# Seven products for eight in the out step of the last 1024 tokens, with a new order for the late third

## The chip, the cores and the metric

The kernel runs on one core of one Trainium2 chip. The metric is the device time of one execution in microseconds. Five engines run their own instruction streams side by side: TensorE (PE in the profile), VectorE (DVE), ScalarE (ACT), GpSimd (POOL) and SyncE (SP, which here only issues DMAs). They wait for one another through semaphores.

## The reference

An attention layer with a forgetting gate feeds a bilinear feed-forward layer. Batch 8, 8 heads, 576 positions, head dimension 64; 4608 tokens of 512 features, 1536 hidden units.

```python
scores = scale * np.matmul(q, k.transpose(0, 1, 3, 2))
cum = np.cumsum(np.log(np.clip(f, 0.0001, 1.0)), axis=-1)
scores = np.where(causal, -1e9, scores + cum[..., :, None] - cum[..., None, :])
attn = softmax(scores)                      # max taken off, summed, + 1e-9
x = np.matmul(attn, v)                      # -> (4608, 512), heads side by side
out = ((x @ w_a) * (x @ w_b)) @ w_out       # (512, 1536), (512, 1536), (1536, 512)
```

Inputs and output are float32; the kernel multiplies in float16 and sums in float32.

## The kernel before, in words

**Attention** goes batch by batch, two heads (a pair) at a time, 32 pairs t = 0 to 31. For a pair TensorE makes the scores into PSUM (tile `sc`), VectorE adds the decay and takes the row's extreme in one instruction (line 673, reading `sc` from PSUM and the tile `spread` from SBUF, writing `S`), ScalarE takes the exponential (700 to 704, tiles `PA` and `PB`), VectorE the reciprocal (712, 714), GpSimd multiplies by it in place (725, float16 in SBUF, the "norms"). SyncE transposes `PA` and `PB` by DMA into `PTA` and `PTB` (739), TensorE multiplies with v (768, 783, `pvx`), and VectorE or ScalarE casts the result into the tiles `xT`, which hold x transposed.

**The feed-forward layer** follows on tokens that are ready. The *in step* of a chunk (`ffn`) makes for each block of 128 hidden units `psa` and `psb` (x with w_a and w_b), ScalarE casts `psa` to `a`, VectorE multiplies (line 1072) to the float16 hidden tile `ht`. The *out step* (`out_step`, `ff_out`) multiplies 128 tokens' hidden tiles with w_out: 12 blocks of hidden units, each as two halves of 64 output rows side by side (line 74, `mm_halves`), 512 columns, into the PSUM tile `pso`. A copy to `osb` and a DMA to the output follow. The last 128 tokens go in three pieces of 256, 128 and 128 columns (`psz`).

**The last 1024 tokens** have another in step already, `winograd()`. Taking two halves of 512 tokens and two halves of the 512 features, x with w_a and w_b forms a two by two block product, done per block of hidden units in seven products of four matmuls of 512 columns (`product`, tiles `wg`, `wb`) for eight. It needs sums of the weights (`sub_w`, line 1218, 12 VectorE instructions on 128x1024 float16) and of x (`add_x`, line 1224, 8 of them on 128x512 float16), copies of partial products to SBUF (`snap`, lines 288 and 292, tiles `wu`, `wv`) and combinations (`combine`, line 1273): c11, c12, h2 and half of the c22 on VectorE, each with one input from PSUM; h1 and the other half of the c22 on GpSimd, both inputs from SBUF. h1 and h2 are the hidden tiles of the two halves of tokens (`hy`, `ht` and `hx`).

**Order.** Nothing is scheduled at run time. Each piece of work is an `Op`; the string `ORDER` lists all of them in the sequence in which they are recorded, which is each engine's instruction order; `CHOICE` names the engine where two could do an operation; `SLOTS` says which buffer of each ring a tile takes. An engine works strictly in its order and stops at an instruction whose inputs or buffer are not ready.

Of the kernel before, what the change touches and what calls it, by code (L numbers as in the profile page):

```python
# [9 lines left out]
FP32 = mybir.dt.float32  # L10
# [15 lines left out]
def kernel(  # L26
# [78 lines left out]
    def paddings():  # L105
# [37 lines left out]
        0110101010101001010101010101010010011010100101001000100010011011010011010100110101001101010101011010110  # L143
        ;a16:012012012012012012012012012012012102102120120120120102102102021021012012012102102102102102;bc:0120
        120120120120120120120120;ff:012301230132000312301201313123131023120221010121332030123012301230123012301
        3021320210123103103023103120321023102310230231032123123120323102103102132012301020201230213201320312031
        0321032102312312031203120123102310231021031231230132132132020310310320120312023102130213210320312031213
        0131030310132102013013012301303210310210310321320320132031023012301231203012301213021031212302301320123
        01320123103210321302130210321013201320;ht:0123456789abcd0123456789abcd0123456789ab01cd2345678a019b23cd4
        568017a29bd345c0168279a34bd015c2;n16:011010010110001010010101010101;n32:0120102102102102010202121220120  # L150
        110102121101202201201202102;nv:01010101;osb:010101010100101010101010101110101010;qd:0101010101010101010
        10101;sc:0101010101010101010101011010010101100010101011001001010110101010101101010101010101010010101110
        1100101010110010101110101010101010100101010101;st:01234510324510324510324510324510
# [41 lines left out]
    def packets(n, size):  # L195
        return n * PKT[size] / 16
# [1077 lines left out]

    PLAIN = range(0, 12, 2)

    def winograd():
# [24 lines left out]
        muls = [[], []]  # L1302
        hu = {}
        first = None
        for fb in range(12):
# [59 lines left out]
    for n in cuts:  # L1365
# [85 lines left out]
        1507-1509 1421 1450 1451 1414 1532 1436 1429 2100 1489 1490 1385 2102 1487 1371 1372 2104 1581 1452  # L1451
# [11 lines left out]
        2161 2159 2143 1691 1692 2211 1587 2162-2164 2166 2165 1649 2167 1543 2209 1530 1693 1602 1550 1594  # L1463
# [3 lines left out]
        1703 2216 2210 2213 2194 1651 1658 2197 2214 2198-2200 2212 1657 1660-1662 1701 1702 1704-1706 2202  # L1467
# [5 lines left out]
        2322 2307-2309 2326 2324 2310 2335 2351 2312 2338 2325 2328 2327 2329 2311 2313 2314 2317 2330 2341  # L1473
        2336 2332 2331 2334 2337 2318 2339 2340 2342 2344 2345 2316 2354 2315 2319 2333 2352 2353 2366 2346
        2355 2356 2369 2343 2357 2358 2348 2349 2347 2350 2372 2373 2360 2359 2367 2368 2363 2382 2361 2370
        2375 2371 2364 2362 2365 2397 2374 2376-2378 2398 2379 2381 2399 2383-2385 2400 2403 2401 2402 2388
        2386 2387 2201 2405 2404 2410 2413 2390 2389 2394 2406 2407 2391 2392 2380 2414 2411 2409 2395 2393
        2408 2415 2416 2418-2420 2417 2421 2423-2426 2422 2396 2428 2427 2412 2429 2430 2433 2434 2431 2432
        2435 2438 2436 2437 2439-2446 2448-2450 2453 2451 2454 2447 2452 2455-2462
# [3 lines left out]
        PPPPPPDDDAPPPPPPPPPAADAAAAADADDAAAAADADDADADDAADDDAADAADDDADADDAAAADADDAADAAADADDAAAAAAADDDAAAAAADAAADA  # L1483
        AAAADADAAAAAADADDAAAAAAADDDAAAAAADAAAAAAADADAAADAAAAAAADADAAAAAAAAA
# [46 lines left out]
```

## Time and profile before

| | |
|---|---|
| median of 3 runs | 397.29 us (396.17 to 397.76) |
| the profiled execution | 395.96 us, span of its instructions 393.9 us |
| granted TensorE clock | 1.00 |
| busy, TensorE / VectorE / ScalarE / GpSimd | 382.3 / 319.2 / 296.5 / 280.4 us |
| first block product of the last 1024 tokens (`wg`) | starts at 332.90 us |
| last matmul | ends near 391 us |

A row of the timeline is: start, duration (of a merged run of like instructions), engine, line, operation, output tile <- input tiles, shape, count, and in brackets the idle time before it and what ended that. A row of a group has the busy time, the mean of one instruction in ns, and the idle time before the group. A row of a table by stretches of time has its limits, its length, and for each engine the busy time with the number of instructions, then the granted clock, the DMA engines' share and GB/s. In the chain of waits, a row is the start, the time on the chain, engine, tile, line and count.

### The profile page before, as it was taken

What the parts mean: (1) busy time and instruction counts of PE and PEld (TensorE: products, weight loads), DVE (VectorE), ACT (ScalarE), POOL (GpSimd) and SP (SyncE); (2) the same over time, 40 slices, a digit from 0 to 9 for tenths busy, and PEclk for the clock granted to TensorE, in tenths of its full rate; (3) what the DMA queues carried; (4) which work ended last, traced back from release to release, by engine and by line L of the source; (5) the groups of instructions that cost most, each with busy time, mean ns of one, the idle gap of its engine ahead of it and who ended that gap; (6) DMA issues with size and microseconds to landing.
All of it is one profiled execution on the core that took longest, in us unless ns stands there. A gap on an engine that the chain in (4) does not pass through costs nothing.

```text
span 393.9 us, 14686 instructions
## 1 busy us (share of the span) xinstructions
PE 382.3 (97%) x5720; PEld 251.3 (64%) x5720; DVE 319.2 (81%) x1015; ACT 296.5 (75%) x817; POOL 280.4 (71%) x482
## 2 busy tenths in 40 slices
PE   7899999999999999999999999999999989999997
PEld 3557977969766665655555665555655677666665
DVE  7888898998997779788887798758998898989700
ACT  4998999999888878778988588789898662455221
POOL 8699677778877689884897779678976980357600
PEclk9999999999999999999999999999999999999999
DMA  7999999999999999999999999999999895100022
GB/s 125 265 188 173 153 147 232 231 289 284 188 233 245 219 285 211 263 236 266 256 229 264 256 227 213 260 270 229 207 203 223 185 139 137 55 1 2 2 108 107
DMA packets 147365, 76.87 MB, mean 195 GB/s; under 512 B 124384, under 2 KB 128352, under 8 KB 147296
## 3 DMA queue, kind: packets, MB, share of 16 engines
q1 hardware_dynamic: 132856, 68.72, 77.2%
q0 software_dynamic: 14256, 7.08, 14.6%
q8 instruction: 44, 0.72, 0.7%
q14 instruction: 25, 0.20, 0.2%
q10 hardware_dynamic: 184, 0.14, 0.1%
HBM read 52.05 MB, written 9.58 MB: 156 GB/s over the span
## 4 chain that ended last, share of the span: by engine, by line
PE 79%; DMA 7%; POOL 4%; DVE 4%; ACT 3%; issue 2%; DVEq 0%; ACTq 0%; POOLq 0%
PE pso L74 20%; PE psa L74 16%; PE psb L74 15%; PE wg L74 5%; PE wb L74 4%; PE sc L550 3%; PE pvx L768 3%; DMA PTB<-PB 2%; PE psT L358 2%; DMA wout<-in_moe_w_out_dram 2%; POOL PA L725 2%; PE sc L538 2%; ACT PA L704 2%; PE wake L74 2%; DVE S L673 2%
## 5 line engine op out<-in xcount | busy, mean ns | idle before, releaser
L673 DVE CUSTOM_DVE_ANT_0 S<-sc,spread 64x576 f32<-64x576 f32 (+4 forms) x232 | 125.4, 561 | 14.2 <-ACT PA L704 4.8
L725 POOL TENSOR_SCALAR PA<-PA,st 128x256 f16<-128x256 f16 (+2 forms) x180 | 85.6, 487 | 10.5 <-DVE st L714 7.5
L74 PE MATMUL psa<-xT,wa 128*64 128x512 f16 (+2 forms) x864 | 88.9, 333 | 1.7 <-DVE ht L1072 1.7
L74 PE MATMUL psb<-xT,wb 128*64 128x512 f16 (+2 forms) x864 | 88.7, 332 | 0.4 <-DVE ht L1072 0.2
L704 ACT ACTIVATE PA<-S,st 128x256 f16<-128x256 f32 (+2 forms) x168 | 84.1, 503 | 6.2 <-DVE st L673 5.7
L74 PE MATMUL pso<-wout,ht 128*64 128x512 f16 x696 | 85.5, 380 | 0.3 <-DMA wout<-in_moe_w_out_dram 0.3
L725 POOL TENSOR_SCALAR PB<-PB,st 128x512 f16<-128x512 f16 (+1 forms) x90 | 64.0, 719 | 23.4 <-DVE st L714 8.7
L74 PEld LDWEIGHTS <-wa 128*64 128x64 f16 x960 | 55.4, 110 | 26.3 <-issue 4.2
L74 PEld LDWEIGHTS <-wb 128*64 128x64 f16 x960 | 56.5, 110 | 24.3 <-issue 1.7
L288 ACT CAST a<-psa 128x512 f16<-128x512 f32 (+1 forms) x90 | 49.4, 551 | 18.1 <-PE psa L74 14.9
L1072 DVE TENSOR_TENSOR ht<-psb,a 128x512 f16<-128x512 f32 (+1 forms) x90 | 57.6, 649 | 6.2 <-PE psb L74 4.1
L74 PEld LDWEIGHTS <-ht 128*64 128x64 f16 x696 | 38.8, 110 | 27.9 <-issue 2.6
L704 ACT ACTIVATE PB<-S,st 128x512 f16<-128x512 f32 x56 | 40.2, 720 | 3.4 <-DVE st L673 2.9
L704 ACT ACTIVATION_READ_ACCUMULATOR PA<-S,st 128x1 f32 x168 | 31.9, 190 | 0.0
L700 ACT ACTIVATE PB<-S,st 128x576 f16<-128x576 f32 x28 | 21.7, 776 | 9.2 <-DMA PTB<-PB 3.6
L630 POOL TENSOR_SCALAR_AFFINE_SELECT spread<-spread 128x768 f32<-128x768 f32 x24 | 20.9, 871 | 10.7 <-DMA spread<-cum_d 10.3
L288 ACT COPY osb<-pso 128x512 f32<-128x512 f32 x28 | 16.3, 583 | 15.4 <-PE pso L74 15.4
L768 PEld LDWEIGHTS <-nv 128*64 128x64 f16 x640 | 22.0, 110 | 6.7 <-DMA PTA<-PA 2.1
L1273 POOL TENSOR_TENSOR hy<-wu 128x512 f16<-128x512 f32 x9 | 11.4, 1278 | 20.3 <-DVE wu L1273 20.3
L673 DVE CUSTOM_DVE_ANT_1 S<-sc,spread 128x256 f32<-128x256 f32 x48 | 19.7, 420 | 6.5 <-PE sc L538 1.9
L714 DVE RECIPROCAL st<-st 128x2 f32<-128x2 f32 x128 | 18.2, 156 | 7.4 <-ACT PA L704 3.8
L673 DVE DVE_READ_ACCUMULATOR2_ANT st<- 128x1 f32 (+1 forms) x280 | 22.9, 82 | 0.0
(136 smaller groups left out, 674.6 us busy)
## 6 DMA issues: line engine op xcount, KB each, us to landing
spread<-cum_d SPq DMA_DIRECT2D x24, 576.0 KB, 6.4
out_dram<-osb SPq DMA_DIRECT2D x35, 256.0 KB, 3.4
q<-in_q_dram SPq DMA_DIRECT2D x14, 576.0 KB, 5.3
k<-in_k_dram SPq DMA_DIRECT2D x14, 576.0 KB, 5.1
v<-in_v_dram SPq DMA_DIRECT2D x24, 256.0 KB, 6.0
wout<-in_moe_w_out_dram POOLq DMA_DIRECT2D x3, 512.0 KB, 8.0
nv<-in_v_dram POOLq DMA_DIRECT2D x8, 128.0 KB, 5.9
wa<-in_moe_w_a_dram POOLq DMA_DIRECT2D x2, 512.0 KB, 7.6
```

Source lines behind the costliest of these rows:

```text
L74: nc.tensor.matmul(out=out[r], lhsT=lhsT[:, r], rhs=rhs, **kw)
L288: nc.scalar.copy(out=out_, in_=in_)
L550: nc.tensor.matmul(out=dst, lhsT=lhsT, rhs=rhs, start=start, stop=stop, skip_group_check=True)
L630: nc.gpsimd.affine_select(out=c[:, :, 0:SM].rearrange("p h (j k) -> p h j k", k=128), in_=c[:, :, SM:2 * SM].rearrange("p h (j k) -> p h j ...
L673: nc.vector.tensor_tensor_reduce(out=o, in0=x, in1=y, scale=-1.0, scalar=3e38, op0=ADD, op1=MIN, accum_out=m)
L700: nc.scalar.activation(out=p_blocks(t, 4), in_=T[("s" if direct else "z", t, 4)], func=EXP, bias=st[:, 8:9], scale=sign, accum_out=st[:, 1 ...
L704: nc.scalar.activation(out=p_blocks(t, i)[:, :, h, :], in_=(T[("s", t, i)][:, h, :] if direct else T[("z", t, i)][:, h * n:h * n + n]).rea ...
L714: nc.vector.reciprocal(out=st[:, 20 + 2 * i:22 + 2 * i], in_=st[:, 10 + 2 * i:12 + 2 * i])
L725: VEC[e].tensor_scalar(out=p, in0=p, scalar1=st[:, c:c + 1], scalar2=1.0, op0=MUL, op1=MUL)
L768: nc.tensor.matmul(out=o[HP[h], 128 * i:128 * i + 128], lhsT=vt[:, j, pr + NP * h, :], rhs=pt[:, base_blk[i] + 2 * block_at(t, i, j) + h, ...
L1072: nc.vector.tensor_tensor(out=ht[:, 0:n_], in0=T.pop(("psb", t0, fbs))[:, 0:n_], in1=T.pop(("a16", t0, fbs))[:, 0:n_], op=MUL)
L1273: VEC[e].tensor_tensor(out=out_, in0=x, in1=y, op=op)
```

## The change

Three things are changed; `winograd()` and the loop over batches stay.

1. The out step of the last 1024 tokens becomes a two by two block product too: two halves of 512 tokens with two halves of the 512 output columns, over even and odd blocks of hidden units. For each of four blocks of 128 tokens (p, standing for a block in each half) there are seven products of 6 x 2 matmuls of 256 columns (`out_product`, Ops `vm1` to `vm7`). The weight differences (`sub_out`, tile `tw`: four of them in two pieces, 128x768 float16) and the sums of hidden tiles (`add_h`, Ops `sh0` to `sh3`: 24 on 128x512 float16, kept in the buffers of `spread` and, for `sh2`, in place) are VectorE's. Partial products are copied to SBUF (`o_snap`, tile `ou`), joined (`o_join`, 12 on 128x256 float32, one input from PSUM), copied (`o_copy`) and stored by rows of 512 columns; the very last block's lower row is stored in two pieces.
2. `out_step` is no longer called for these tokens, and the three-piece end (`last_out`) is gone with it.
3. `ORDER`, `CHOICE` and `SLOTS` are new from the softmax of pair 26 on. In `CHOICE`, three casts of `pvx` and two copies of `pso` go from VectorE to ScalarE, one copy of `kT` the other way, and in the last stage seven copies of partial products from VectorE to ScalarE.

```diff
+    def sub_out(e, k, j):
+        fs = slice(3 * j, 3 * j + 3)
...
+        t = [T[("tw", m)][:, fs, :] if ("tw", m) in T else None for m in range(4)]
+        x, y = ((w_out(0, fs, 1), w_out(0, fs, 0)), (w_out(1, fs, 1), t[0]),
+                (w_out(1, fs, 1), w_out(0, fs, 1)), (w_out(1, fs, 0), t[1]))[k]
+        VEC[e].tensor_tensor(out=t[k], in0=x, in1=y, op=SUB)
...
+    def add_h(e, k, f):
+        h = lambda i, j: T[("ht", TW[i], 2 * f + j)]
+        x, y = ((h, (1, 0)), (h_sum, (0, f)), (h, (0, 0)), (h, (0, 1)))[k], ((h, (1, 1)), (h, (0, 0)), (h, (1, 0)), (h_sum, (1, f)))[k]
+        x, y = x[0](*x[1]), y[0](*y[1])
+        VEC[e].tensor_tensor(out=h_sum(k, f), in0=x, in1=y, op=SUB if k else ADD)
+
+    def out_product(m, p):
...
+        for f in range(6):
+            x = {1: lambda: T[("ht", TW[0], 2 * f)], 2: lambda: T[("ht", TW[0], 2 * f + 1)], 3: lambda: h_sum(3, f),
+                 4: lambda: T[("ht", TW[1], 2 * f + 1)], 5: lambda: h_sum(0, f), 6: lambda: h_sum(1, f),
+                 7: lambda: h_sum(2, f)}[m]()[:, c]
...
+            mm_halves(o, x, w, start=(f == 0 and m in (1, 2, 5)), stop=(f == 5), skip_group_check=True)
...
+            m1 = mm(1, [])
+            s1 = cp(1)
+            m2 = mm(2, [])
+            j11 = join(11, [m2, s1])
+            m5 = mm(5, [])
+            s5 = cp(5)
+            m6 = mm(6, [s1])
+            s6 = cp(6)
+            m3 = mm(3, [s5])
+            j12 = join(12, [m3, s6, j11])
...
+            au.append(store(0, 0, 512, [j11, j12]))
+            m7 = mm(7, [s6])
+            j22 = join(22, [m7, s5])
...
+            m4 = mm(4, [j22])
...
-                muls[half].append((h, hu[key]))
-        for tb in range(8):
-            out_step(TW[0], tb, muls[tb // 4], 0.04 * TW[0])
+                hids[(half, fb)] = (h, hu[key])
+        out_products(hids)
```

VectorE's instructions in the last stage, before. L1273 are the combinations, L292 copies of partial products, L1218 the last weight difference of the in step.

```order
L1273 TENSOR_TENSOR hx<-wg,wv 128x512
L1218 TENSOR_TENSOR wb_77<-wb_77 128x2x512
L292 COPY wv<-wb 128x512
L1273 TENSOR_TENSOR wu<-wb,wu 128x512 x3
L1273 TENSOR_TENSOR wv<-wv,wg 128x512
L1273 TENSOR_TENSOR hx<-wg,wv 128x512 x2
L1273 TENSOR_TENSOR wu<-wb,wu 128x512 x2
L292 COPY wu<-wg 128x512
L1273 TENSOR_TENSOR wu<-wb,wu 128x512
```

The same place now. L1299 are the sums of hidden tiles; they read `hx`, `hy` and `spread`, all in SBUF.

```order
L1273 TENSOR_TENSOR hx<-wg,wv 128x512
L1299 TENSOR_TENSOR spread_85<-hx 128x512
L1273 TENSOR_TENSOR wu<-wb,wu 128x512
L1273 TENSOR_TENSOR hx<-wg,wv 128x512
L1273 TENSOR_TENSOR wu<-wb,wu 128x512
L1273 TENSOR_TENSOR wv<-wv,wg 128x512
L1299 TENSOR_TENSOR spread_86<-spread_85,hy 128x512
L1273 TENSOR_TENSOR wu<-wb,wu 128x512
L1273 TENSOR_TENSOR wv<-wv,wg 128x512
L1273 TENSOR_TENSOR wu<-wb,wu 128x512 x2
L1273 TENSOR_TENSOR hx<-wg,wv 128x512 x2
L1299 TENSOR_TENSOR spread_85<-hx 128x512
```

The copies have gone to ScalarE, and hidden sums stand between the combinations. GpSimd's list in this stage is still 12 h1 and 6 c22.

In the late third, VectorE's end of the softmax of pair 31 and of the plain in step, before (L1072 the hidden products, L673 the decay, here named ISA, whose second row reads its extreme out):

```order
L673 ISA S,st<-sc_7687,spread_84 64x576
L673 ISA st 64x1
L1218 TENSOR_TENSOR xT_73<-wb_77,xT_72 128x2x512
L1072 TENSOR_TENSOR ht<-psb,a_7759 128x384
L1072 TENSOR_TENSOR ht<-psb,a_7798 128x384
L1218 TENSOR_TENSOR xT_72<-wb_77,wa_76 128x2x512
L1072 TENSOR_TENSOR ht<-psb,a_7856 128x384
```

And now (L1286 the differences of w_out):

```order
L1072 TENSOR_TENSOR ht<-psb,a_7757 128x384
L1072 TENSOR_TENSOR ht<-psb,a_7779 128x384
L1072 TENSOR_TENSOR ht<-psb,a_7812 128x384
L1286 TENSOR_TENSOR tw<-wout_78 128x768
L1218 TENSOR_TENSOR xT_73<-wb_77,xT_72 128x2x512
L712 RECIPROCAL st<-st 128x1
L673 ISA S,st<-sc_7850,spread_86 128x512
L673 ISA st 128x1
L673 ISA S,st<-sc_7850,spread_86 128x512
```

From pair 26 on, three w_out differences and two L1218 stand ahead of the softmax's last reciprocal (L714) now, where three L1218 stood before; the other five w_out differences come behind it.

More of the change, by code (lines that the diff above doesn't have):

```diff
@@ L147 @@
[L147 to L151, printed above, removed]
@@ new lines @@
+        1230130213202101231031030231031203210231023102302310321231230123130210230210312013202121201321031203123
+        0123023102310213013012301230120130213021302102301301320310310312123023023120123012130210321031023123012
+        3010320302323020310212032032103123130213210213213023013012301321031203120313201302130132013023231302130
+        23203123012302032012031203103210321033212;ht:0123456789abcd0123456789abcd0123456789ab01cd2345678a019b23
+        cd4568017a29bd345c0168279a34bd015c2;n16:011010010110001010010101010101;n32:0120102102102102010202121220
@@ L154 @@
+        1201101021211012012012012012010211;nv:01010101;osb:01010101010010101010101011000010;qd:0101010101010101
+        01010101;sc:0101010101010101010101011010010101100010101011001001010110101010101101010101010101010010101
+        11011001010101100101011011010101010101010101010101011;st:01234510324510324510324510324510
     """
@@ L1273, in combine, with w_out @@
         VEC[e].tensor_tensor(out=out_, in0=x, in1=y, op=op)
+    def w_out(k, fs, c):
+        return wout16.rearrange("p (f k) c -> p f k c", k=2)[:, fs, k, 256 * c:256 * c + 256]
+    def sub_out(e, k, j):
+        fs = slice(3 * j, 3 * j + 3)
+        if ("tw", k) not in T:
+            T[("tw", k)] = qkT_pool.tile([128, NP, S], FP16, tag=("qT", "kT")[k % 2], name="tw").rearrange(
+                "p a s -> p (a s)")[:, 0:1536].rearrange("p (f c) -> p f c", f=6)
+        t = [T[("tw", m)][:, fs, :] if ("tw", m) in T else None for m in range(4)]
+        x, y = ((w_out(0, fs, 1), w_out(0, fs, 0)), (w_out(1, fs, 1), t[0]),
+                (w_out(1, fs, 1), w_out(0, fs, 1)), (w_out(1, fs, 0), t[1]))[k]
+        VEC[e].tensor_tensor(out=t[k], in0=x, in1=y, op=SUB)
@@ new lines, in h_sum @@
+    def h_sum(k, f):
+        if k == 2:
+            return T[("ht", TW[1], 2 * f)]
+        if ("sh", k) not in T:
+            T[("sh", k)] = turn(("bc", ("sh", k)), "bc", spread).rearrange("p h s -> p (h s)").bitcast(FP16)
+        return T[("sh", k)][:, 512 * f:512 * f + 512]
+    def add_h(e, k, f):
[3 more added lines that the diff above has]
+        VEC[e].tensor_tensor(out=h_sum(k, f), in0=x, in1=y, op=SUB if k else ADD)
@@ new lines, in o_snap, with o_row @@
+    def o_snap(e, m, p):
+        if m == 1:
+            T[("ou", p)] = slot(n32_pool, [128, 2 * TG * 64], FP32, "n32", "ou")
+        c = 256 * {1: 0, 6: 1, 5: 2}[m]
+        cast(e, T[("ou", p)][:, c:c + 256], T[("om" if m == 5 else "og", p)][:, 0:256], False)
+    def o_row(p, half):
+        if ("or", p, half) not in T:
+            T[("or", p, half)] = (slot(s_pool, [128, 1024], FP32, "S", "or") if half else
+                                  slot(osb_pool, [128, 512], FP32, "osb", "osb"))
+        return T[("or", p, half)]
@@ new lines, in o_join, with o_copy, o_store @@
+    def o_join(e, what, p):
+        u = T[("ou", p)]
+        x, y, o = {11: lambda: (T[("ob", p)], u[:, 0:256], o_row(p, 0)[:, 0:256]),
+                   12: lambda: (T[("om", p)], u[:, 256:512], o_row(p, 0)[:, 256:512]),
+                   22: lambda: (T[("og", p)], u[:, 512:768], o_row(p, 1)[:, 256:512])}[what]()
+        VEC[e].tensor_tensor(out=o, in0=x[:, 0:256], in1=y, op=ADD)
+    def o_copy(e, p, lo, hi):
+        cast(e, o_row(p, 1)[:, lo:hi], T[("og", p)][:, lo:hi], False)
+    def o_store(e, p, half, lo, hi):
+        r0 = TW[half] + 128 * p
+        (nc.scalar if e == "ACT" else nc.sync).dma_start(out=out[r0:r0 + 128, lo:hi], in_=o_row(p, half)[:, lo:hi])
```

120 lines of the change are left out of this document (100 added, 20 removed), and 49 rows, old and new, of the table ORDER.

## The prediction

> **What bounds the kernel now.** I read the busy shares first, then PE's waits over the whole run, then the end of the chain of waits, then the last stage's busy time by engine.
>
> ```profile
> PE 382.3 (97%) x5720; PEld 251.3 (64%) x5720; DVE 319.2 (81%) x1015; ACT 296.5 (75%) x817; POOL 280.4 (71%) x482
> PE psa L74 <- DVE ht L1072: 1.7, 1, 1.7
> 371.95 16.40 PE pso L74 x152
> 388.35 2.67 PE psz L74 x72
> core 0: us, PE busy (x) PEld busy (x) DVE busy (x) ACT busy (x) POOL busy (x), PEclk, DMA share, GB/s
> 333.00:372.00 39.00, 39.00 (x366) 25.76 (x362) 34.68 (x58) 18.66 (x34) 21.48 (x18) 1.00 0.05 19
> 372.00:394.00 22.00, 19.00 (x224) 13.27 (x220) 1.66 (x3) 4.74 (x9) 1.19 (x1) 1.00 0.26 96
> ```
>
> TensorE sets the time: 382.3 of 393.9 us busy at full granted clock, with one wait over 1.5 us in the late third (1.7, on the DVE product that frees a PSUM buffer). From 333 to 372 us, the block products of the in step, it streams without a gap; from 372 to the end it does the out step, while DVE works 1.66 us of 22. But the second engine is close behind: DVE is busy 34.68 of the 39 us before 372. Those two rows are the whole case. The change takes work from PE's last 20 us and gives work to DVE, most of it in the 39 us in which DVE has 4.3 us left.
>
> **TensorE's part.** The old out step is 192 matmuls of 512 columns (8 token blocks, 12 blocks of hidden units, two halves). The chain's row has 152 in 16.40 us, 0.108 each, so 192 cost 20.7. The new one is 4 x 7 products of 12 matmuls of 256 columns: 336 at half of 0.108, 18.1 us. **Saved: 2.6 us.** Are narrow matmuls as cheap per column? The psz row holds 24 of 256 and 48 of 128 columns in 2.67 us; at 0.054 and 0.027 each they would take 2.59. The excess is 0.08 us on 72, so 0.4 us on 336: the saving lies between 2.2 and 2.6. Nothing else on PE is added; I take 2.6.
>
> **VectorE's part in the last stage.** Prices:
>
> ```profile
> L1273 DVE TENSOR_TENSOR wu<-wb,wu 128x512 f32<-128x512 f32 x24 | 16.3, 686 | 2.9 <-ACT wv L288 0.7 <-PE wb L74 0.6 <-ACT wu L288 0.5
> L1224 DVE TENSOR_TENSOR xT<-xT,xT 128x512 f16<-128x512 f16 x5 | 2.0, 417 | 0.0
> 333.02 0.76 DVE L1224 TENSOR_TENSOR xT<-xT 128x512 f16<-128x512 f16 x2
> 340.62 0.68 DVE L1273 TENSOR_TENSOR hx<-wg,wv 128x512 f16<-128x512 f32 x1
> 341.22 0.68 DVE L1273 TENSOR_TENSOR wu<-wb,wu 128x512 f32<-128x512 f32 x1
> 335.96 0.69 DVE L1273 TENSOR_TENSOR wu<-wb,wu 128x512 f32<-128x512 f32 x1 [0.31 <-ACT wv L288]
> 332.90 1.06 PE L74 MATMUL wg<-xT,wa 128*64 128x512 f16 x8
> L1273 POOL TENSOR_TENSOR hy<-wu 128x512 f16<-128x512 f32 x9 | 11.4, 1278 | 20.3 <-DVE wu L1273 20.3
> L1273 POOL TENSOR_TENSOR wv<-wv 128x512 f32<-128x512 f32 x6 | 7.7, 1276 | 2.3 <-ACT wv L288 1.8 <-DVE wv L292 0.5
> L1273 POOL TENSOR_TENSOR ht<-wu 128x512 f16<-128x512 f32 x3 | 3.8, 1276 | 2.8 <-DVE wu L1273 2.7
> ```
>
> A 512-wide instruction occupies DVE 0.60 us from start to start (340.62 to 341.22), whatever its recorded 0.68; a 16-bit 512-wide sum 0.34 (0.76 less 0.42 for the second of two). The new order has, from the first combination to the last hidden sum, 42 combinations and 2 copies (0.60), two weight differences (0.60), 24 hidden sums and one 256-wide copy (0.34): 27.6 + 8.5 = 36.1 us. Seven 512-wide copies go to ScalarE, which was busy 18.66 of 39. DVE's first combination stood 3.1 us after the stage began (335.96 against 332.90), and DVE idled 4.3 us in it for others' results, so its last hidden sum would be done at about 3.1 + 36.1 + 4.3 = 43.5. TensorE needs it for the first of the four seventh products of the out step, which in the new order stands behind all 84 in-step products of four matmuls (36.2) and ten new ones of 0.65 (6.5): at 42.7. The two meet within a microsecond: **the plan has no slack on DVE**, so what holds a hidden sum up holds TensorE.
>
> **What holds them up.** The hidden sums, the four w_out differences (tw) and the older weight differences (L1218) are alike in one thing: both inputs lie in SBUF. The combinations read one input from PSUM. Here is what the L1218 rows show when GpSimd works at the same time:
>
> ```profile
> 289.61 0.87 DVE L1218 TENSOR_TENSOR xT<-wb,wa 128x1024 f16<-128x1024 f16 x1
> 313.06 2.92 DVE L1218 TENSOR_TENSOR xT<-wb,xT 128x1024 f16<-128x1024 f16 x1
> 316.96 0.68 DVE L1218 TENSOR_TENSOR xT<-wb,wa 128x1024 f16<-128x1024 f16 x1
> 324.81 0.87 DVE L1218 TENSOR_TENSOR xT<-wb,wa 128x1024 f16<-128x1024 f16 x1
> 289.26 1.79 POOL L725 TENSOR_SCALAR PB<-PB,st 128x512 f16<-128x512 f16 x2 [0.76 <-DVE st L714]
> 312.86 1.27 POOL L725 TENSOR_SCALAR PA<-PA,st 128x384 f16<-128x384 f16 x3
> 314.09 0.40 POOL L637 TENSOR_SCALAR_AFFINE_SELECT spread<-spread 128x256 f32<-128x256 f32 x1
> 314.48 0.58 POOL L725 TENSOR_SCALAR PA<-PA,st 128x384 f16<-128x384 f16 x1
> 315.02 0.40 POOL L637 TENSOR_SCALAR_AFFINE_SELECT spread<-spread 128x256 f32<-128x256 f32 x1
> 315.41 0.92 POOL L725 TENSOR_SCALAR PA<-PA,st 128x256 f16<-128x256 f16 x1
> 318.27 1.28 POOL L725 TENSOR_SCALAR PA<-PA,st 128x128 f16<-128x128 f16 x3 [1.94 <-DVE st L714]
> 321.71 3.44 POOL L725 TENSOR_SCALAR PB<-PB,st 128x576 f16<-128x576 f16 x5
> ```
>
> The same instruction takes 0.68 with GpSimd idle (316.96; its row at 318.27 shows 1.94 us of idle before it), but 0.87, 2.92 and 0.87 when it starts inside a GpSimd row. At 324.81 it ends 0.53 after GpSimd's 325.15; at 313.06 it lives through six GpSimd instructions, ends at 315.98, and the one that GpSimd starts at 315.41 takes 0.92 for some 0.5. I read that as: the two exclude each other, and the later one waits. This also explains PE's 1.7 us wait, just behind 313.06. The Trainium skill says the same (SBUF — State Buffer, Who interferes with whom): a VectorE instruction with two SBUF inputs and a GpSimd one that reads SBUF share a read interface, and the second to issue is blocked until the first is done. By that rule 313.06 should have waited for one instruction, not six; the rows decide, and a wait can be longer than the rule's.
>
> No row of before shows a hidden sum beside the GpSimd products of L1273, so the price is bounded. GpSimd's 18 of these cost 23.0 us; in 42.7 us that is a share of 0.54. An add that meets one waits 0.64 us on average, half of 1.28: 24 x 0.54 x 0.64 = 8.3 us. Below: 0, every sum in a gap of GpSimd. Above: twice that, 16.6, where it also loses one hand-over, as at 313.06. DVE's 4.3 idle us can absorb part: **I take +5.5**, between 8.3 - 4.3 = 4.0 and 8.3.
>
> **The late third.** DVE gets eight tw differences of 768 columns, which no row shows; between 0.34 for 512 and 0.60 for 1024 (326.07 to 326.67 below), about 0.48 each, 3.8 us.
>
> ```profile
> 326.07 0.68 DVE L1218 TENSOR_TENSOR wb<-wb 128x1024 f16<-128x1024 f16 x1
> 326.67 0.68 DVE L1218 TENSOR_TENSOR xT<-wb,xT 128x1024 f16<-128x1024 f16 x1
> L292 DVE CAST xT<-pvx 128x576 f16<-128x576 f32 x4 | 2.9, 752 | 0.2 <-PE pvx L783 0.2
> L292 DVE COPY osb<-pso 128x512 f32<-128x512 f32 x3 | 2.0, 681 | 1.3 <-PE pso L74 1.3
> ```
>
> It loses three pvx casts and two osb copies to ScalarE and takes back one 576-wide copy, about -2.6. So its work grows by 1.2 us. Before, four L1218 instructions started before GpSimd's last norm ended (325.15) and waited 0.19 + 2.24 + 0 + 0.19 = 2.6 us, of which PE felt 1.7. Now about seven stand there (four of them tw): at the mean of 0.66 each, 4.6 us, 2.0 more, of which PE feels two thirds. With the added work partly in DVE's gaps **I take +1.5**. Bounds: -1.7, the old stall goes and nothing comes; +8.6, all seven wait like 313.06 (7 x 2.24 - 2.6 = 13.1, two thirds felt). The moved scores, transposes and loads issue the same instructions; I cost their order at nothing, covered by PE's queue of in- and out-step matmuls; the 1.7 us is what a lost cover cost here.
>
> **The tail.** Before, the last copy is 128 columns wide and the last store 64 KB. Now it is a 256-wide sum and 256 KB. The wv row serves the second rival.
>
> ```profile
> 388.15 2.84 PE L74 MATMUL psz<-wout,hx 128*64 128x256 f16 x72
> 391.09 0.29 DVE L292 COPY osb<-psz 128x128 f32<-128x128 f32 x1 [17.17 <-PE psz L74]
> L288 ACT COPY wv<-wg 128x512 f32<-128x512 f32 x5 | 2.9, 587 | 5.1 <-PE wg L74 5.1
> out_dram<-osb SPq DMA_DIRECT2D x12, 256.0 KB, 2.0
> out_dram<-osb SPq DMA_DIRECT2D x1, 64.0 KB, 1.6
> ```
>
> The sum is 0.42 (between 0.29 for 128 and 0.68 for 512), the landing 2.0 for 1.6: **+0.5**.
>
> **Sum**, against the profiled execution's span of 393.9 (395.96 around it, 1.3 under the median of 397.29): -2.6 + 5.5 + 1.5 + 0.5 = +4.9, a span of 398.8. On the median: **402.2 us**.
>
> **Rivals.** (1) The hidden sums slip into GpSimd's gaps. For it: GpSimd works 21.48 of 39 us and mostly waits for DVE itself, so an in-order DVE may often find it idle. Against it: the hidden sums stand among the combinations that set GpSimd going. Then -2.6 + 0.5 and 0 to -1.7 in the late third: 395.2 to 393.5, faster. It decides where the sums' waits stay under 2 us in all. (2) Only the hand-over costs. Behind the last seventh in-step product stand a copy, GpSimd's c22, h2 and one hidden sum in a row, 0.59 (ScalarE's wv row) + 1.28 + 0.69 + 0.42, and 0.1 for each of five hand-overs (388.15 + 2.84 to 391.09): 3.5 us, against 3.2 of products ahead of the first fifth product (three in-step ones of 0.43, three new ones of 0.65). A second such row, c12 to GpSimd's h1 to the third product, is as tight. Some 1.2 us in all, without any exclusion: -2.6 + 1.2 + 0.5 = -0.9, 396.4. Against its being all: it leaves out the waits that 313.06 shows. (3) GpSimd's unbroken norms starve DVE in the late third, as at 313.06, each time: -2.6 + 5.5 + 8.6 + 0.5, 409.3. Against it: two of three waits were short.
>
> **Chances.** Forecast 0.55, with its own range 399 to 407 (late third 0 to 4, sums 4 to 8.3); (1) 0.20; (2) 0.13; (3) 0.12. A measurement of this kernel can tell about 0.5% from no change, 395.3 to 399.3. Faster is most of (1): 0.18. Same is the rest of it, most of (2) and the forecast's low edge: 0.20. Slower 0.62. The range of 8 in 10 runs from 394 into (3): 394 to 409.
>
> **What would show it.** Right: L1299 rows far over 0.42 us whenever a GpSimd L1273 row covers their start, L1286 rows over 0.55, PE waits on DVE inside the in-step products that before had none, and an out step of 18 us of matmul. Wrong: L1299 rows all near 0.42, or long ones while PE still streams; then (1). If the PE waits lie only behind the last in-step product it is (2); if most lie before the first wg, (3).

## The result: 0.6% slower, and the profile after

| | before | after |
|---|---|---|
| median of 14 runs each, side by side | 396.68 us | 400.21 us |
| ratio of the times, 95% interval | | 1.0062 (1.0036 to 1.0088) |
| the profiled execution / its span | 395.96 / 393.9 us | 400.72 / 399.0 us |
| first `wg` of the last stage starts | 332.90 us | 336.58 us |
| from there to the last matmul's end | 58.09 us | 58.92 us |
| from the last matmul's end to the span's end | 2.9 us | 3.5 us |

The ratio leaves out the slow executions, those over 1.5% above the fastest of the same kernel, which is why it is smaller than that of the two medians. The direction was forecast, the size was not: +0.62% where +1.24% was forecast. The profiles are read in the same order as before: busy shares, TensorE's waits, the last stage. First the changed kernel's busy shares, and its last stage in the table by stretches (columns as in the prediction).

```profile
PE 382.3 (96%) x5816; PEld 254.6 (64%) x5816; DVE 334.7 (84%) x1052; ACT 301.8 (76%) x830; POOL 284.4 (71%) x482
336.58:395.50 58.92, 56.48 (x674) 41.76 (x670) 51.58 (x94) 26.35 (x53) 23.55 (x18) 1.00 0.09 33
```

The same stage of the kernel before, and a piece of its stream in the timeline:

```profile
332.90:391.00 58.10, 58.10 (x586) 39.13 (x582) 36.14 (x60) 23.40 (x43) 22.67 (x18) 1.00 0.12 46
335.92 1.06 PE L74 MATMUL pso<-wout,ht 128*64 128x512 f16 x8
```

Before, TensorE was busy the whole stage. VectorE's busy time in it grew from 36.1 to 51.6 us. What would the new stage take without a stall? The eight `pso` matmuls at 335.92 run ahead of the stage in the new order (8 x 0.108 = 0.86), the old out step of 20.7 us goes, and 28 products of 12 matmuls come. One takes 0.65 us from start to start, here in the changed kernel's timeline:

```profile
393.37 0.82 PE L74 MATMUL og<-tw,hx 128*64 128x256 f16 x12
394.02 1.48 PE L74 MATMUL om<-wout,spread 128*64 128x256 f16 x24
```

So 58.09 - 0.86 - 20.7 + 28 x 0.65 = 54.7 us. The stage took 58.92: **4.2 us of stall**, more than the 2.5 us that the products save. The largest stalls, in TensorE's timeline of the changed kernel:

```profile
361.59 0.41 PE L74 MATMUL wg<-xT 128*64 128x512 f16 x2 [0.36 <-DVE wv L1273]
369.46 0.62 PE L74 MATMUL wb<-xT,wb 128*64 128x512 f16 x4 [0.70 <-DVE wu L1273]
374.62 0.41 PE L74 MATMUL wg<-xT 128*64 128x512 f16 x2 [0.35 <-DVE wv L1273]
382.97 0.74 PE L74 MATMUL om<-wout,spread 128*64 128x256 f16 x10 [0.83 <-DVE spread L1299]
```

All wait for VectorE. Taken from start to start, these four rows delay the stream by 0.56, 0.90, 0.55 and 1.02 us, 3.0 of the 4.2; the rest is in smaller delays. Three of the four lie inside the in-step products, where the kernel before had none. What held VectorE up is in the rows of the sums of hidden tiles: the view of line 1299 of the changed kernel (shortest, median and longest in ns, first and last start).

```profile
L1299 DVE TENSOR_TENSOR spread<-hx x6: 416/810/1307, 347.3 to 377.7; 128x512 f16<-128x512 f16 x6
L1299 DVE TENSOR_TENSOR spread<-spread,hy x5: 410/425/1375, 350.5 to 374.5; 128x512 f16<-128x512 f16 x5
L1299 DVE TENSOR_TENSOR hx<-hy,hx x5: 407/411/1494, 366.7 to 382.8; 128x512 f16<-128x512 f16 x5
```

Seven of the 24 took 0.80 to 1.49 us, the others 0.41 to 0.43; above 24 x 0.41 they lost 5.5 us. The timeline of VectorE beside GpSimd's suggests why:

```profile
351.99 1.27 DVE L1273 TENSOR_TENSOR wu<-wb,wu 128x512 f32<-128x512 f32 x2
354.50 1.04 DVE L1299 TENSOR_TENSOR spread<-hx 128x512 f16<-128x512 f16 x1
355.64 0.42 DVE L1299 TENSOR_TENSOR spread<-spread,hy 128x512 f16<-128x512 f16 x1
366.72 1.49 DVE L1299 TENSOR_TENSOR hx<-hy,hx 128x512 f16<-128x512 f16 x1
380.83 0.41 DVE L1299 TENSOR_TENSOR spread<-ht,spread 128x512 f16<-128x512 f16 x1
352.75 2.51 POOL L1273 TENSOR_TENSOR hy<-wu 128x512 f16<-128x512 f32 x2 [2.64 <-DVE wu L1273]
355.75 1.46 POOL L1273 TENSOR_TENSOR wv<-wv 128x512 f32<-128x512 f32 x1 [0.49 <-POOL hy L1273]
366.55 1.38 POOL L1273 TENSOR_TENSOR hy<-wu 128x512 f16<-128x512 f32 x1 [1.31 <-DVE wu L1273]
379.25 1.38 POOL L1273 TENSOR_TENSOR ht<-wu 128x512 f16<-128x512 f32 x1 [2.26 <-DVE wu L1273]
```

Each of the seven starts inside a GpSimd row and ends 0.28 us after it: 366.72 + 1.49 = 368.21, and GpSimd's 366.55 + 1.38 = 367.93; 354.50 + 1.04 = 355.54, and 352.75 + 2.51 = 355.26. It goes the other way too: GpSimd's 355.75 starts inside the sum of 355.64 and takes 1.46 for its usual 1.28. The two combinations at 351.99, with one input from PSUM, run straight through GpSimd's start at their usual 1.27 for two. After GpSimd's last row (ends at 380.63) no sum waits. The Trainium skill's rule (SBUF — State Buffer, Who interferes with whom), that the second of the two to issue is fully blocked until the first is done, fits these seven rows, each of which waits only for the GpSimd instruction that is running; that a wait lives through several instructions, as at 313.06 in the kernel before, is not seen here.

Two more places answer steps of the prediction. In the late third, the view of line 1286, a row of VectorE's timeline and one of TensorE's, all of the changed kernel:

```profile
L1286 DVE TENSOR_TENSOR tw<-wout x4: 542/647/950, 311.6 to 326.6; 128x768 f16<-128x768 f16 x4
309.76 1.20 DVE L1218 TENSOR_TENSOR xT<-wb,wa 128x1024 f16<-128x1024 f16 x1
335.17 0.25 PE L768 MATMUL pvx<-PTB,nv 128*64 128x128 f16 x2 [1.26 <-DMA PTB<-PB]
```

The longest wait there is 0.5 us (1.20 for 0.68, at 309.76); the 1.73 us stall of before is gone, and one of 1.26 us on a transpose has come. And early in the program, where nothing was changed, the first profile of after loses about 2 us between 40 and 60 us (TensorE busy 17.78 of 20, DVE and ACT less busy too); all later marks are 3 us late. The table by stretches of after, and below it of before:

```profile
40.00:60.00 20.00, 17.78 (x398) 14.98 (x398) 15.34 (x62) 16.88 (x50) 14.15 (x19) 1.00 1.25 144
```

```profile
40.00:60.00 20.00, 19.73 (x430) 16.68 (x426) 18.40 (x73) 19.19 (x59) 14.34 (x20) 1.00 1.39 148
```

Without these 3 us the profiles differ by +2.1 us: -0.1 in the late third (in before 70.64 us from the `sc` row at 262.26 to the first `wg`, plus the moved 0.86, so 71.50; in after 71.36 from the same row at 265.22), +1.7 in the last stage, +0.6 after it. That is 0.5%, and the ratio says 0.62 with 0.36 to 0.88.

### The profile page after: what moved, and what is told of

Its sections match the earlier page's. It is cut to its first block, busy times and chain, and to the rows that moved or that the text cites. A ratio compares the mean times of both kernels' runs of the same rounds, so it can differ in the third digit from the quotient of the medians.

```text
span 399.0 us, 14929 instructions
## 1 busy us (share of the span) xinstructions
PE 382.3 (96%) x5816; PEld 254.6 (64%) x5816; DVE 334.7 (84%) x1052; ACT 301.8 (76%) x830; POOL 284.4 (71%) x482
## 4 chain that ended last, share of the span: by engine, by line
PE 75%; POOL 7%; DVE 6%; DMA 5%; issue 4%; ACT 2%; POOLq 0%; ACTq 0%; DVEq 0%
PE psa L74 15%; PE pso L74 15%; PE psb L74 15%; PE sc L550 4%; PE wg L74 4%; POOL PA L725 3%; DMA PTB<-PB 3%; PE psT L358 3%; PE pvx L768 3%; PE wb L74 3%; PE og L74 2%; PE sc L538 2%; PE psP L74 2%; PE wake L74 2%; POOL PB L725 2%
## 5 line engine op out<-in xcount | busy, mean ns | idle before, releaser
L673 DVE CUSTOM_DVE_ANT_0 S<-sc,spread 64x576 f32<-64x576 f32 (+4 forms) x232 | 125.7, 561 | 16.4 <-ACT PA L704 4.8
L725 POOL TENSOR_SCALAR PA<-PA,st 128x384 f16<-128x384 f16 (+2 forms) x180 | 87.1, 493 | 12.2 <-DVE st L714 5.7
L74 PE MATMUL pso<-wout,ht 128*64 128x512 f16 x672 | 82.3, 380 | 0.0
L74 PEld LDWEIGHTS <-wb 128*64 128x64 f16 x960 | 56.2, 110 | 26.8 <-issue 4.1
L74 PEld LDWEIGHTS <-wa 128*64 128x64 f16 x960 | 55.5, 110 | 25.3 <-issue 2.9
L1072 DVE TENSOR_TENSOR ht<-psb,a 128x512 f16<-128x512 f32 (+1 forms) x90 | 57.5, 648 | 6.8 <-PE psb L74 4.9
L673 DVE CUSTOM_DVE_ANT_1 S<-sc,spread 128x256 f32<-128x256 f32 x48 | 19.6, 418 | 7.0 <-PE sc L538 2.5
L1273 POOL TENSOR_TENSOR hy<-wu 128x512 f16<-128x512 f32 x9 | 11.5, 1289 | 18.4 <-DVE wu L1273 18.4
L288 ACT COPY wu<-wg 128x512 f32<-128x512 f32 x24 | 13.8, 589 | 11.9 <-PE wg L74 8.3
L673 DVE DVE_READ_ACCUMULATOR2_ANT st<- 128x1 f32 (+1 forms) x280 | 22.7, 81 | 0.0
L714 DVE RECIPROCAL st<-st 128x2 f32<-128x2 f32 x128 | 18.2, 156 | 4.9 <-ACT PA L704 2.3
```

Of the source, the lines that this page charges most:

```text
L74: nc.tensor.matmul(out=out[r], lhsT=lhsT[:, r], rhs=rhs, **kw)
L288: nc.scalar.copy(out=out_, in_=in_)
L673: nc.vector.tensor_tensor_reduce(out=o, in0=x, in1=y, scale=-1.0, scalar=3e38, op0=ADD, op1=MIN, accum_out=m)
L714: nc.vector.reciprocal(out=st[:, 20 + 2 * i:22 + 2 * i], in_=st[:, 10 + 2 * i:12 + 2 * i])
L725: VEC[e].tensor_scalar(out=p, in0=p, scalar1=st[:, c:c + 1], scalar2=1.0, op0=MUL, op1=MUL)
L1072: nc.vector.tensor_tensor(out=ht[:, 0:n_], in0=T.pop(("psb", t0, fbs))[:, 0:n_], in1=T.pop(("a16", t0, fbs))[:, 0:n_], op=MUL)
```

## The experiments

Theory A: the loss is made in the last stage, by sums of hidden tiles shut out while GpSimd reads SBUF. Rivals: the loss lies elsewhere (the beginning, the new late third), or VectorE's added load is to blame, whatever it meets.

**Both kernels once more.** No edit.

> The kernel before, unchanged, for a second profile. In the changed kernel's profile the first common place of both programs after 60 us, a score product that stood at 87.84 us, came 3.07 us later, and that lag was still 2.96 at 262 us, where the two programs are still the same instructions. Theory A: the lag is scatter of the first 50 us between executions; then the two profiles of before may differ there by some 0 to 3 us as well, and from 60 to 270 us by under 0.5. Theory B: the lag belongs to the changed program; then the two profiles of before agree within 0.5 us everywhere ahead of the late third.

> The changed kernel, unchanged, for a second profile and for timing beside the others. Theory A (scatter in the first 50 us): the lag against before at a common place near 262 us is anything from 0 to 3 us. Theory B (the lag belongs to the change): again 2.5 to 3.5. Both: the same seven hidden sums (L1299) of 24 over 0.75 us, TensorE's stalls between the first wg and the last matmul 3.5 to 5 us, time 0.4 to 0.9% over before.

Measured: before 395.63 us, one run; after 399.83 us, ratio 1.0083 (1.0055 to 1.0111). The last stage repeats: 58.09 us in before, 58.93 in after, the same seven long sums. The late third of before does not: TensorE's wait on `ht` was 0.38 us this time where it was 1.73, in its timeline here, and from the `sc` row (at 263.64) to the first `wg` (at 332.93) it took 69.29 us for 70.64.

```profile
316.66 0.84 PE L74 MATMUL psa<-xT,wa 128*64 128x384 f16 x8 [0.38 <-DVE ht L1072]
```

With the moved 0.86 that is 70.15, and the changed kernel took 71.73 in this profile, with a wait of 1.59 us on the same transpose. So what its late third costs is -0.1 us against one execution of before and +1.6 against the other. The lag at the `sc` row is scatter, as theory A said: the row stood at 262.26 and 263.64 in before, at 265.22 and 264.46 in after. The pause between 40 and 60 us was there in this profile of after, and in none of before. What follows: the stage's loss belongs to the program; whether the pause does was left to later runs.

**GpSimd's products read almost nothing.** In this kernel GpSimd's h1 and c22 compute 8 of 512 columns and fill the rest with zeros, so the result is not the reference's; GpSimd is held somewhat longer, but nearly all of it by writes.

```diff
+        if e == "POOL":
+            nc.gpsimd.tensor_tensor(out=out_[:, 0:8], in0=x[:, 0:8], in1=y[:, 0:8], op=op)
+            for c0, c1 in ((8, 512), (8, 512), (392, 512)):
+                nc.gpsimd.memset(out_[:, c0:c1], 0.0)
+            return
```

> The changed kernel in which GpSimd computes 8 of the 512 columns of its h1 and of its half of the c22 and fills the rest with zeros in three writes of about the same total length, so its hidden tiles hold zeros there. It waits for the same inputs, but nearly all of its time reads nothing. Theory A (a VectorE sum with both inputs in SBUF and a GpSimd instruction that reads SBUF exclude each other): all 24 hidden sums at 0.41 to 0.6 us, 5.4 us of waiting gone, TensorE's stalls in the last stage down from 4.3 to about 0.5 us, time 3 to 4 us under the changed kernel, so 0.3 to 0.6% under before. Theory B (the sums are long for their place, or any GpSimd work delays them): seven sums still near 0.8 to 1.5 us and the time that of the changed kernel within 1 us. A third way (only the hand-over): sums short or long, the stalls behind the last in-step product stay (1 us and more), time 1 us under the changed kernel at most.

Measured: 393.81 us, ratio 0.9965 (0.9918 to 1.0011). Its last stage, its sums (line 1304 here) and two places of its timeline:

```profile
337.14:392.45 55.31, 55.18 (x674) 41.96 (x670) 46.92 (x94) 26.39 (x53) 24.91 (x72) 1.00 0.10 35
L1304 DVE TENSOR_TENSOR spread<-hx x6: 415/426/453, 347.9 to 375.6; 128x512 f16<-128x512 f16 x6
L1304 DVE TENSOR_TENSOR hx<-hy,hx x5: 409/418/424, 366.4 to 379.8; 128x512 f16<-128x512 f16 x5
366.37 0.42 DVE L1304 TENSOR_TENSOR hx<-hy,hx 128x512 f16<-128x512 f16 x1
366.20 0.31 POOL L1274 TENSOR_TENSOR hy<-wu 128x8 f16<-128x8 f32 x1 [1.10 <-DVE wu L1278]
366.46 1.35 POOL L1276 MEMSET hy<- 128x504 f16 x3
```

The sum at 366.37 is the one that took 1.49 in the changed kernel; beside GpSimd's writes it takes 0.42. All sums are short, and the stage is 55.31 us, 3.6 less, with the same instructions on VectorE and TensorE and the same order. The load theory falls: VectorE's instructions are the same. Of the 4.2 us of stall 3.6 come from GpSimd's reads, 0.6 remain, most of it ahead of the last in-step product. That a GpSimd instruction that only writes does not block is also what the Trainium skill's section named above states, and these rows agree.

**The new late third alone.** The kernel before with the changed kernel's order, engines and buffers up to the first `wg`, without the `tw` differences, and with the old out step.

```diff
     SLOTS = """
-        0110101010101001010101010101010010011010100101001000100010011011010011010100110101001101010101011010110
...
+        0101010110110101010100101001;n16:011010010110001010010101010101;ff:01230123013200031230120131312313102
...
```

> The kernel before with the changed kernel's order, engines and buffers up to the first in-step product of the last 1024 tokens, without the differences of w_out; from there on the old order and the old out step. Theory A (the cost sits in the last stage; from the two profiles the late third, its common lag taken off, came out at -0.1 us with one out-step piece moved into it): the same as before within 0.7 us. Theory B (my prediction: the late third costs too): 1 to 2 us over before. If the new late order were the main cost: 2.5 us and more over before.

Measured: 396.17 us, ratio 1.0001 (0.996 to 1.0043).

```profile
261.40:332.13 70.73, 69.32 (x969) 43.19 (x965) 58.08 (x194) 54.65 (x154) 53.17 (x94) 1.00 0.98 205
```

Two rows of its TensorE timeline:

```profile
330.72 0.25 PE L768 MATMUL pvx<-PTB,nv 128*64 128x128 f16 x2 [1.32 <-DMA PTB<-PB]
335.64 0.62 PE L74 MATMUL wg<-xT,wb 128*64 128x512 f16 x4 [0.30 <-ACT wu L288]
```

From the `sc` row to the first `wg` 70.73 us, with the 0.86 moved in: between the 71.50 and 70.15 of before's two profiles. The wait on the transpose, which neither profile of before has, comes with the new order. The moved `pso` piece is missed where it stood: a wait on a copy makes the old last stage 57.72 us, 0.5 more than 58.09 - 0.86. Together the new order alone costs nothing that can be seen. That does not settle the +1.5 us: the interval is 0.4%, 1.6 us, either way, and the `tw` differences, part of that term, are not in this kernel.

**Other places for the sums.** Two kernels with the changed kernel's instructions and another `ORDER` (moved3 also has one GpSimd product at another place), and one of them with a cut last store. Through a slip in the last, the early piece stores another row block's columns, so 128 rows by 256 columns stay unwritten; the transfers have the sizes meant.

```diff
-        2145 1673 1677 1679 1678 1600 2149 1680 2147 2150 2152 2154 2156 1686 1669 2153 1515 1685 2207 1647
-        2413 1648 1529 1572 2143 1616 1516 2155 1530 1681 1631 1683 1668 2157 1649 2158-2162 2164 2151 2165
...
+        2145 1673 1677 1679 1678 1600 2149 1680 2147 2150 2152 2154 2156 1686 1669 2153 1515 1685 1647 1648
+        1529 1572 2143 1616 1516 2155 2413 1530 1681 2207 1631 1683 1668 2157 1649 2158-2162 2164 2151 2165
...
```

> The changed kernel with its order alone altered: the same instructions on every engine, GpSimd's, ScalarE's and TensorE's in the same sequence, and 41 of VectorE's operations at other places (differences of the down weights, sums of hidden tiles, last combinations, joins), so that the sums of hidden tiles (L1299) are issued in GpSimd's gaps or after its last row. Theory A (what the change costs is VectorE's sums being shut out while a GpSimd product reads memory): all 24 L1299 rows at 0.41 to 0.45 us where 7 of 24 took 0.8 to 1.5, TensorE's stalls in the last stage down from 4.3 us to 1 or less, so 3 to 4 us under the changed kernel: 396 to 397 us, and with the 2.6 us of saved products now kept, a ratio to the kernel before of 0.993 to 0.999. Theory B (the stage is set by VectorE's added load, 24 sums of 0.41 us and 16 more joins and copies, whatever they meet): waits move to other places, time 399 to 401. For the beginning of the program: as this kernel has the changed kernel's length but another order, idle time of TensorE with nothing waited for between 40 and 60 us of 2 us or more would belong to the longer program; none would make it one execution's chance.

> The kernel of the run moved2, and in it the last row block that TensorE finishes is stored in two pieces: columns 0 to 255 from ScalarE's queue as soon as they are joined, columns 256 to 511 after the last join, so that the transfer that ends last carries 128 KB in place of 256 KB. The span after TensorE's last matmul was 3.5 us in the changed kernel and 2.9 in the kernel before, whose last transfer carried 64 KB (256 KB took 2.0 us from issue to landing, 128 KB 1.7, 64 KB 1.6). Expected from that: 0.3 us under moved2 in the span, not to be told apart in the time: ratio 0.992 to 0.998 if theory A holds.

> As moved2, another such order (48 operations at other places, one of them a product of GpSimd). Theory A: the same as moved2, 396 to 397 us and all L1299 rows at 0.41 to 0.45; two orders that both avoid the meetings should agree within 1 us. Theory B: 399 to 401, and the two would differ by where the load falls.

Measured: moved2 396.02 us, ratio 1.0 (0.9961 to 1.0039); moved2_split 397.84, 1.004 (1.0001 to 1.0078); moved3 394.64, 0.9975 (0.9939 to 1.0011). A ratio between 0.993 and 0.999, as expected, came in moved3 alone. The last stage of moved2, and its longest `tw` row:

```profile
331.84:388.74 56.90, 55.62 (x674) 41.73 (x670) 48.80 (x95) 26.17 (x53) 23.13 (x18) 1.00 0.09 34
341.89 1.65 DVE L1286 TENSOR_TENSOR tw<-wout,tw 128x768 f16<-128x768 f16 x1
```

The last stage of moved3, and the sums that still wait there:

```profile
332.55:388.90 56.35, 55.39 (x674) 42.02 (x670) 48.46 (x95) 26.27 (x53) 23.14 (x18) 1.00 0.10 35
350.28 1.16 DVE L1299 TENSOR_TENSOR spread<-hx 128x512 f16<-128x512 f16 x1
367.16 0.93 DVE L1299 TENSOR_TENSOR spread<-hx 128x512 f16<-128x512 f16 x1
369.20 0.41 PE L74 MATMUL wg<-xT 128*64 128x512 f16 x2 [0.69 <-DVE wv L1273]
```

Theory A holds in direction: the same instructions at other places, and the stage is 2.0 and 2.6 us shorter. But "all 24 at 0.41 to 0.45" was not reached: a few sums still met GpSimd, and in moved2 a `tw` did (1.65 for 0.54). The stall that is left, 2.2 and 1.6 us, goes with what is still lost in meetings. The slip in the cut store has a price of its own, seen in that kernel's timeline:

```profile
389.61 0.42 DVE L1334 TENSOR_TENSOR osb<-ob,ou 128x256 f32<-128x256 f32 x1 [3.43 <-DMA out_dram<-osb]
```

The last block's join waits until the misdirected store has read its buffer, and the stretch after the last matmul is 4.8 us in place of 3.6; this run says nothing on the cut.

None of these three profiles has the pause at 40 to 60 us, though their program is as long as the changed kernel's; that of gp_writes has (TensorE busy 16.52 of the 20 us).

**The loss once more, and two more steps.** The changed kernel unchanged; moved3 with four sums moved on VectorE (its order before and after, with - and +); and both orders with the last store cut, this time rightly.

```diff
 L1273 TENSOR_TENSOR hx<-wg,wv 128x512 x2
+L1273 TENSOR_TENSOR wu<-wb,wu 128x512
 L1299 TENSOR_TENSOR spread_85<-hx 128x512
 L1299 TENSOR_TENSOR spread_86<-spread_85,hy 128x512
-L1273 TENSOR_TENSOR wu<-wb,wu 128x512 x2
+L1273 TENSOR_TENSOR wu<-wb,wu 128x512
...
 L1273 TENSOR_TENSOR hx<-wg,wv 128x512
+L1273 TENSOR_TENSOR wv<-wv,wg 128x512
+L1273 TENSOR_TENSOR wu<-wb,wu 128x512
+L1273 TENSOR_TENSOR hx<-wg,wv 128x512 x2
 L1299 TENSOR_TENSOR spread_85<-hx 128x512
 L1299 TENSOR_TENSOR spread_86<-spread_85,hy 128x512
-L1273 TENSOR_TENSOR wv<-wv,wg 128x512
-L1273 TENSOR_TENSOR wu<-wb,wu 128x512
-L1273 TENSOR_TENSOR hx<-wg,wv 128x512 x2
```

```diff
-            au.append(store(0, 0, 512, [j11, j12]))
+            au.append(store(0, 256 if p == 2 else 0, 512, [j11, j12]))
+            if p == 2:
+                last = (au, j11)
...
+        last[0].append(Op("ACT", 0.53, lambda e: o_store(e, 2, 0, 0, 256), [last[1]], land=packets(128, 1024)))
```

> The changed kernel unchanged, on the same chip and beside the same runs of the kernel before as the three below. Theory A (the loss is made in the last stage): from the start of the in-step's first product to the end of the last matmul 58.7 to 59.1 us, seven sums of hidden tiles far over 0.42 us, ratio to the kernel before 1.005 to 1.009. Of the beginning of the program: its two profiles so far show 2.1 us of TensorE idle with nothing waited for between 40 and 60 us, which no profile of the kernel before or of the run moved2 shows. If that belonged to the program in every execution, the ratio would be about 1.011 (2.2 us from the last stage and 2.1 from here, over 397); if the timed executions do not have it, 1.006.

> The kernel of the run moved3 with four sums of hidden tiles moved once more on VectorE: two that waited there (1.16 us at 350.28, 0.93 at 367.16) go behind the combination L1273 that followed, and behind the next four. Theory A: these two at 0.41 to 0.65, TensorE's wait of 0.69 us for L1273's wv at 369.20 gone, the stage from the in-step's first product to the last matmul's end 55.5 to 56.2 us where moved3 had 56.31: ratio 0.993 to 0.999. Theory B: no change beyond 0.2 us in the stage.

> The kernel of the run moved4, with the store of the row block that TensorE finishes last cut in two: columns 0 to 255 from ScalarE's queue, columns 256 to 511 from SyncE's after the last join, so 128 KB land last in place of 256 KB. From the landings of such pieces (256 KB 2.0 us, 128 KB 1.7) 0.3 us less after the last matmul: 3.2 us in place of 3.5. Ratio 0.992 to 0.998.

> The kernel of the run moved3 with the same cut of the last store: 3.2 us after the last matmul in place of 3.5, the rest as moved3, ratio 0.992 to 0.999.

Measured: after_third 398.38 us, ratio 1.0043 (1.0006 to 1.008); moved4 398.14, 1.0016 (0.998 to 1.0051); moved4_split 396.55, 0.9995 (0.9964 to 1.0026); moved3_split 394.49, 0.9941 (0.9911 to 0.997).

The changed kernel's stage was 58.95 us, the third time within 0.03; its ratio lies just under the expected 1.005 to 1.009. The pause was not there; it was in the profile of moved4. The stretch of after_third, then that of moved4 with its last stage and two meetings:

```profile
40.00:60.00 20.00, 19.79 (x436) 16.59 (x430) 18.10 (x70) 19.11 (x59) 14.16 (x19) 1.00 1.42 152
```

```profile
40.00:60.00 20.00, 18.13 (x406) 15.29 (x406) 15.80 (x62) 17.45 (x52) 14.18 (x19) 1.00 1.27 145
335.53:393.26 57.73, 55.80 (x674) 41.91 (x670) 49.06 (x95) 26.24 (x53) 23.14 (x18) 1.00 0.09 34
354.75 1.46 DVE L1299 TENSOR_TENSOR spread<-hx 128x512 f16<-128x512 f16 x1
377.66 1.50 DVE L1299 TENSOR_TENSOR spread<-hy,spread 128x512 f16<-128x512 f16 x2
354.66 1.27 POOL L1273 TENSOR_TENSOR wv<-wv 128x512 f32<-128x512 f32 x1 [0.52 <-ACT wv L288]
377.16 1.38 POOL L1273 TENSOR_TENSOR ht<-wu 128x512 f16<-128x512 f32 x1 [2.22 <-DVE wu L1273]
```

So the pause comes and goes with the execution, and the same program has both. moved4 and moved4_split missed their expectations: 57.73 and 57.74 us for 55.5 to 56.2, and ratios above those expected. The two sums that had waited were short of it, but the shift made others start 0.1 us behind a GpSimd product (354.75 against 354.66) and inside another (377.66). Where a sum stands in the list decides what it meets only together with everything ahead of it.

The cut of the last store did what was expected: 392.04 us to the span's end of 395.2 is 3.2 us in moved3_split, against 3.5 in moved3.

**The best version again.** No edit to moved3_split.

> The kernel of the run moved3_split once more, unchanged. Its ratio of 0.9941 (0.9911 to 0.997) is below what its last stage gives against the kernel before: 57.23 us there (58.09 less the pso piece of 0.86 that the other order runs before the stage) against 56.32, and 3.16 us after the last matmul against 2.9: together 0.65 us, 0.9984. If the stage is all, this run is at 0.996 to 1.000; if the late third of this order brings something too, 0.992 to 0.996.

Measured: 393.90 us, ratio 0.9912 (0.988 to 0.9944).

```profile
334.08:390.38 56.30, 55.38 (x674) 41.95 (x670) 48.46 (x95) 26.25 (x52) 23.15 (x18) 1.00 0.10 36
```

It is faster than the kernel before in two series of runs, by 0.6 and 0.9%. The last stage explains little of that: it is the same 56.3 us, and together with the 3.2 us after it, that gives 0.9984, above both intervals. Its late third was 70.80 and 70.31 us in its two profiles (from the `sc` row, first at 264.92, to the first `wg`), before's 71.50 and 70.15, so whether it gains there is open. Where most of the gain comes from is not shown.

What was lost in meetings (sums above 0.41 each, and `tw` rows above 0.54, in the last stage) beside the stage's length:

| kernel | lost by VectorE | last stage | over 54.7 |
|---|---|---|---|
| after, three profiles | 5.5 us | 58.92 to 58.95 | 4.2 |
| moved4 | 2.4 | 57.73 | 3.0 |
| moved2 | 2.4 | 56.90 | 2.2 |
| moved3 | 1.6 | 56.31 | 1.6 |
| GpSimd writes only | 0.2 | 55.31 | 0.6 |

The stage falls with the loss; moved4 and moved2, with the same loss and 0.8 us between their stages, show that the place counts too. That TensorE feels only what comes when its queue is short is a reading, which no run tried.

## Why the prediction was right in direction and too large

Two terms of the sum were too large, the waits of the hidden sums and the late third. In the first the mechanism was right and the size wrong; in the second the path was wrong as well.

- **TensorE's saving, -2.6:** 28 x 0.65 = 18.2 for 20.7, so -2.5. Right.
- **Waits of the hidden sums, +5.5:** the mechanism was right, shown by the writes-only run; the term measured 4.2 us, three times. The step that failed is "24 x 0.54 x 0.64 = 8.3 us" of waits. Seven of the 24 sums stand behind GpSimd's last product, where nothing can meet; of the other 17, at the share of 0.54, nine should have met one, and seven did. Each cost 0.78 us and not 0.64, because on average 0.91 us of the GpSimd product was left: in all 5.5. Of this 3.6 us reached TensorE, so 1.9 were absorbed, where the choice of 5.5 out of 8.3 allowed 2.8. The other 0.6 of the 4.2 is no exclusion: it stays when GpSimd only writes, and what makes it is not shown.
- **"A wait can be longer than the rule's":** the upper end, 16.6 us, with a lost hand-over each time, had no support in the seven meetings: each waited for the one GpSimd instruction that was running. Why 313.06 lived through six was not tried and stays open.
- **The late third, +1.5:** two steps failed here. "Seven stand there, at the mean of 0.66 each" counted on another 313.06 in the mean. Eleven started before GpSimd's last norm ended (330.85); they lost 2.1 us in all, 0.5 the most, against 2.6 before, and no wait of TensorE's over 0.3 us there was ended by VectorE, where two thirds were to be felt. And "I cost their order at nothing" left out the wait on a transpose that the new order brings, 1.26 to 1.59 us in three profiles of the changed kernel. The net is -0.1 us against a profile of before with the 1.73 us stall and +1.6 against the one with 0.38, so the base of "two thirds felt" was itself one execution's chance. The times leave little for it: 0.62% is 2.5 us, and 2.3 of that are the last stage and what follows it. Its exact size stays open.
- **The tail, +0.5:** 3.5 us for 2.9. Right.
- **The sum:** -2.5 + 4.2 - 0.1 + 0.6 = +2.2 us by the first two profiles, 0.55%; measured 0.62%, and 0.83 and 0.43% in the later series. Forecast +4.9. Of the 2.7 us between them, 1.3 are the sums and 1.6 the late third, less 0.2 for the saving and the tail; with the late third as uncertain as said, that the total fits so closely is partly luck.
- **The rivals:** (1), the sums in GpSimd's gaps, is not what this order does, but moved3 comes near it: with the sums mostly in the gaps, the condition "waits under 2 us in all" was met in its last stage (1.6), and its time was 0.9975 (0.9939 to 1.0011), which fits a small gain and does not show one. (2), the hand-over, put 1.2 us of waits behind the last in-step product; without GpSimd's reads 0.1 us of delay is left there. Its two rows, each 3.5 against 3.2, come to 0.6 and not 1.2. (3), starved norms, did not occur; its 8.6 should read 8.7.
- **The signs:** long L1299 rows wherever a GpSimd row covered their start, `tw` over 0.55 (0.95 at most), and PE waits inside in-step products all came. The two profiles alone would have misled: 3 us of the 5.1 between their spans is the lag from the early part, while the timed executions differ by 2.5 us.

## What to carry to other kernels

When a change hands an engine work that shares a read path with another engine, count the meetings: only those instructions that can overlap the other's rows, times the share of time that those rows cover, times what is left of one; then ask how long the waiting engine's customers can go on. Work out the two sides separately, since 2.6 us of a 58.9 us stage went with the position of instructions alone. Cost a new order of transposes too, and take a second profile of the kernel before: its one long stall in the late third was 1.73 us in one execution and 0.38 in the other. And compare stages between marks, not spans: two profiles can differ by 3 us in a part that was never touched.

## What the runs showed of the hardware that was not expected

- The last stage repeats to 0.03 us between executions (58.92, 58.93, 58.95; 56.90 and 56.90; 57.73 and 57.74), while the early part of one and the same program does not: TensorE was busy 17.78 of the 20 us from 40 to 60 in one profile of the changed kernel and 19.79 in another. The cause was not found.
- GpSimd is blocked as VectorE is: its product at 355.75, started 0.11 us into a sum, took 1.46 us for 1.28.
- Three fills of zeros by GpSimd (504, 504 and 120 columns on 128 partitions, 1.35 us together) hold it as long as the product that they replaced (1.28), yet cost VectorE nothing.
